# A planner that counts the memory port shared by VectorE and GpSimd, and the last four attention units of batch 0 split from PSUM

## The chip, the cores and the metric

The kernel runs on one core of one Trainium2 chip. The metric is the device time of one execution in microseconds (us). The engines are TensorE (PE, with its weight loads PEld), VectorE (DVE), ScalarE (ACT), GpSimd (POOL) and SyncE (SP), which issues every DMA here. PSUM is the memory into which PE writes; POOL doesn't reach it.

## What is computed

Clustered attention feeds two layers of two matrix products each, all in fp32 (1536 tokens, model width 512, inner width 2048):

```python
# q, k, v: (2, 8, 768, 64); centroids: (8, 16, 64)
q_assign = argmax(q_n @ c_n); k_assign = argmax(k_n @ c_n)      # normalised rows
scores = where(q_assign == k_assign, scale * q @ k.T, -1e9)
x = softmax(scores) @ v                    # to (1536, 512)
h = x @ w_in;   x = (max(h, 0) + alpha * min(h, 0)) @ w_out
h = x @ w_in2;  out = (h * clip(h + 3, 0, 6) / 6) @ w_out2
```

## The kernel before

**High and low halves.** To keep fp32 accuracy, operands are split in a rounded high part and a remainder: a copy to the narrower type writes the high part, a subtraction writes the low part, and a product is three passes of PE. The copies are on ACT, sometimes on DVE; the subtractions are on POOL where the source is in SBUF, and on DVE where it is in PSUM.

**Attention.** A batch (768 tokens) is done by itself: four pairs of heads (p), two heads (j) each, and six units (t) of 128 queries per head, so 48 units per batch. A pair is first prepared: q and k are loaded and transposed by PE (L461), split by ACT and DVE (L472 to L496), multiplied with the centroids (L518), and on DVE and POOL (L531 to L566) turned into the one-hot cluster codes (eq, oh, lg) that SP writes into the operands (L581). V is scaled and split (L590 to L627). A unit then is: scores by PE into a PSUM pair ps (L662), the row limit by DVE (L669), exp by ACT into the SBUF buffer e (L694), high part by ACT (L728), low part by POOL (L732), both transposed by a DMA (turn, L640) into a buffer pt or, in batch 0 only, half an acc buffer, and the product with V by PE (pv, L647). After a pair, xn is made by DVE (L747) and transposed by PE (L759) into x. Two variants exist: every unit of batch 0 with t % 4 == 2 is transposed by PE (L707) and split from PSUM; and in batch 1 the units with t % 3 != 0 do exp in place in PSUM (L676) and are split from there (L681 on ACT, L685 on DVE), without e.

From unit EARLY = 44 of batch 0 on a unit is "late": it takes e from a ring of one buffer, since the four others lie in a pool that is closed to make room for the weights.

**The two layers.** Each batch goes through both layers: products with w_in (L892, into pb or pc), an activation (L900 to L915), a split into g (L918 on ACT, L922 on POOL), products with w_out (L941, L944), sums by DVE (L952 to L970). For batch 0 each weight block of 128x512 arrives as the two words of a 64-bit number (wd) and is turned into fp32 in a buffer wf (two of them) by ACT (L807) and three DVE steps (L812, L819, L825); it is stored to DRAM for batch 1 (L830), copied (L834, ACT) and subtracted (L839, POOL) into w.

**The order.** All of this is written as operations with an engine (or two to choose from, `pick`), a cost in us, the buffers that they read, write and take, and a due time vt. `Planner.plan` (L102) runs them through a list schedule with one clock: at each moment an idle engine takes the ready operation of the smallest (vt, n) whose buffers are free. The result is one fixed order per engine; on the chip each engine follows its own order and waits only for its inputs. An operation with two engines goes to the second only if the first is taken and has at least BACKLOG = 3 operations ready.

```python
U0, PREP0, SPAN0 = 2.2, -23.969, 15.768
T1, DU, PREP1, SPAN1 = 110.562, 3.672, -22.219, 20.627
```

These set the due times: a unit of batch 0 every U0, the layers of batch 0 and the units of batch 1 from T1 on. The attention of batch 1 thus runs between the products of the layers of batch 0, and the layers of batch 1 come last.

Of the kernel before, what the change touches and what calls it, by code (L numbers as in the profile page):

```python
# [27 lines left out]
LOOK = 0  # L28
EARLY = 44
# [32 lines left out]
class Op:  # L62
    __slots__ = ("eng", "dma", "lat", "fn", "vt", "n", "deps", "soft", "outs", "souts", "acq", "rel", "start", "at")


class Planner:
# [7 lines left out]
    def op(self, eng, cost, fn, r=(), w=(), acq=(), vt=0.0, lat=0.2, dma=0.0, after=()):  # L74
        o = Op()
        o.dma = dma
# [25 lines left out]
    def plan(self):  # L102
# [21 lines left out]
        began = set()  # L124
        soon = {e: [] for e in engines}
# [30 lines left out]
        while events:  # L156
            now = events[0][0]
            while events and events[0][0] <= now:
# [7 lines left out]
                for b in ev.rel:  # L166
                    left[id(b)] -= 1
                    if not left[id(b)]:
                        b.ring.live -= 1
                        for a in b.ring.slots[b.slot][1]:  # L170
                            del busy[a]
                            freed[a] = now
            for e in engines:
                if free_at[e] > now:
                    continue
# [3 lines left out]
                while ready[e]:  # L179
# [4 lines left out]
                    if ahead is not None and ahead < o.vt:  # L184
                        put_back.append(item)
                        break
# [24 lines left out]
                    free_at[e] = now + o.eng[e]  # L211
                    seq += 1
# [21 lines left out]
def kernel(  # L234
# [36 lines left out]
    op = P.op  # L271
# [154 lines left out]
    def pick(engs, costs, fn, **kw):  # L426
        o = op(engs, costs, None, **kw)
# [4 lines left out]
    def attention(b, vt_unit, vt_prep, put_x):  # L432
# [3 lines left out]
        def prep(p):  # L436
# [17 lines left out]
            for nm in "qk":  # L454
# [12 lines left out]
                for j in range(2):  # L467
                    a, z = slice(64 * j, 64 * j + 64), slice(64 - 64 * j, 128 - 64 * j)
                    s = st[j]
                    if nm == "q":  # L470
# [12 lines left out]
                        pick(("ACT", "DVE"), (0.84, 0.8), f, r=[(s["qa"], "h"), (s["qa"], "l")],  # L483
                             w=[(s["qb"], "h"), (s["qb"], "m")], vt=v0 + span * 0.5)
                    else:
# [11 lines left out]
                        pick(("ACT", "DVE"), (0.84, 0.8), f, r=[(s["ka"], "h")], w=[(s["ka"], "h2")], vt=vt)  # L497
# [47 lines left out]
            op("DVE", 0.8, f, r=[(lg, 0), (lg, 1), (mx, 0)], w=[(eq, 0)], acq=[eq], vt=vt, lat=0.13)  # L545
# [11 lines left out]
            op("DVE", 0.8, f, r=["desc", (mx, 1)], w=[(eq, 0)], vt=vt, lat=0.13)  # L557
# [11 lines left out]
            for j in range(2):  # L569
                z = slice(64 - 64 * j, 96 - 64 * j)  # L570
                for x, o in (("qb", 32 * j), ("kb", 64 + 32 * j)):
                    if b == 0 and p == 0:
# [4 lines left out]
                        pick(("ACT", "DVE"), (0.84, 0.8), f, r=[(lg, 0), (lg, 1)], w=[(st[j][x], "m")], vt=vt)  # L577
# [46 lines left out]
            pick(("ACT", "DVE"), (0.84, 0.8), f, r=[(vr, 0), (vr, 1)], w=[(v16, 0)], acq=[v16], vt=vt)  # L624
# [3 lines left out]
            pick(("POOL", "DVE"), (1.7, 1.2), f, r=[(vr, 0), (vr, 1), (v16, 0)], w=[(v16, 1)], vt=vt)  # L628
            vts[p] = (v16, vs)

        def head(p, j, vt0):
# [21 lines left out]
            for t in range(NT):  # L653
# [19 lines left out]
                if b and t % 3:  # L673
# [14 lines left out]
                    op("DVE", 0.97, f, r=[ps, (hl, 0)], w=[(hl, 1)], vt=vt)  # L688
# [371 lines left out]
```

## Time and profile before

| what | value |
|---|---|
| median of 3 runs | 831.65 us (825.08 to 832.09) |
| profiled execution, its own time | 829.24 us |
| its span | 827.5 us |
| mean granted TensorE clock | 0.961 of full speed |
| PE, PEld busy | 750.6 us (91%), 694.5 us (84%) |
| DVE, ACT, POOL busy | 522.4 (63%), 470.9 (57%), 482.1 us (58%) |
| DMA | 121.17 MB, 146 GB/s over the span |

The span runs from the first to the last instruction of the profiled execution; its own time has 1.7 us more around it. Busy shares are means over stages of different kinds. PEclk is the share of full speed that TensorE was granted: 1.00 is 2.4 GHz and 0.50 is 1.2 GHz.

### The profile page before, as it was taken

To read this page: it belongs to the slowest core of one execution; us is meant where nothing else is said; L and a number is where in the kernel's file an instruction comes from. 1 tells how busy PE (TensorE), PEld (TensorE's weight loads), DVE (VectorE), ACT (ScalarE), POOL (GpSimd) and SP (SyncE) were. 2 spreads that over 40 slices of the span, in tenths; PEclk is the share of its full clock that TensorE was granted. 3 is DMA by queue.
4 is the path that set the end of the run, shared out by engine and by line. 5 is a ranking of instruction groups with operands and counts; after the bars stand their busy time and mean duration, and the time that the engine had idled before them with its cause. 6 is when DMAs were issued, how large, how long until landed. Compare 5 with 4: busy or idle time off the path is not lost.

```text
span 827.5 us, 14300 instructions
## 1 busy us (share of the span) xinstructions
PE 750.6 (91%) x5337; PEld 694.5 (84%) x5337; DVE 522.4 (63%) x880; ACT 470.9 (57%) x767; POOL 482.1 (58%) x453
## 2 busy tenths in 40 slices
PE   5667877669999989989999999899999999999997
PEld 4556766659999978889889988789999999899986
DVE  7997888879898888988986888621122222122222
ACT  6777859667576676676665554544433254443421
POOL 3685686846654474654764665675565477564630
PEclk9988898859999999998999999999999999999999
DMA  6599989797789999699995564643222131221201
GB/s 131 118 173 217 173 162 197 123 254 191 193 209 230 183 223 235 118 225 206 207 233 183 181 183 160 181 129 111 64 77 63 43 86 51 64 73 55 77 9 69
DMA packets 212965, 121.17 MB, mean 146 GB/s; under 512 B 169504, under 2 KB 189984, under 8 KB 212896
## 3 DMA queue, kind: packets, MB, share of 16 engines
q1 hardware_dynamic: 212896, 120.26, 62.0%
q8 instruction: 41, 0.67, 0.3%
q14 instruction: 28, 0.23, 0.1%
HBM read 61.38 MB, written 21.50 MB: 100 GB/s over the span
## 4 chain that ended last, share of the span: by engine, by line
PE 53%; DVE 19%; DMA 11%; ACT 7%; issue 5%; POOL 4%; SPq 2%; POOLq 0%; ACTq 0%; DVEq 0%
PE pc L892 12%; PE pb L892 9%; PE pb L941 6%; PE pc L941 6%; PE pb L944 6%; PE pc L944 4%; DVE wf L819 4%; PE ps L662 3%; DMA pt<-hl 3%; DVE wf L825 3%; DVE junk L669 3%; PE ps L518 2%; DMA wd<-in_moe_w_in_dram 2%; DMA wd<-in_moe_w_out_dram 2%; DVE wf L812 2%
## 5 line engine op out<-in xcount | busy, mean ns | idle before, releaser
L839 POOL TENSOR_TENSOR w<-wf,w 128x512 fp32r<-128x512 f32 x128 | 168.5, 1319 | 155.2 <-ACT w L834 100.5
L922 POOL TENSOR_TENSOR big<-t,big 128x384 fp32r<-128x384 f32 x128 | 137.8, 1081 | 82.1 <-ACT big L918 76.5
L892 PE MATMUL pc<-xh,w 128*128 128x384 f32 x544 | 150.7, 338 | 1.8 <-DVE vs L613 1.8
L892 PE MATMUL pb<-xh,w 128*128 128x384 f32 x480 | 133.0, 338 | 0.6 <-DVE t L904 0.6
L834 ACT CAST w<-wf 128x512 fp32r<-128x512 f32 x124 | 76.4, 618 | 88.4 <-DVE wf L825 43.0
L732 POOL TENSOR_TENSOR hl<-e,hl 128x768 f16<-128x768 f32 x56 | 96.6, 1732 | 49.6 <-ACT hl L728 40.0
L892 PEld LDWEIGHTS pc<-xh,w 128*128 128x128 f32 x544 | 99.6, 187 | 2.5 <-DVE vs L613 2.1
L669 DVE TENSOR_SCALAR_CACHE_REDUCE junk<-ps 128x768 bf16<-128x768 f32 x96 | 91.0, 948 | 8.9 <-PE ps L662 5.6
L892 PE MATMUL pc<-xl,w 128*128 128x384 f32 x272 | 91.7, 337 | 0.0
L892 PEld LDWEIGHTS pb<-xh,w 128*128 128x128 f32 x480 | 87.8, 188 | 0.9 <-DVE t L904 0.8
L918 ACT CAST big<-t 128x384 fp32r<-128x384 f32 x125 | 63.6, 512 | 42.0 <-DVE t L913 22.8
L944 PE MATMUL pb<-w,big 128*128 128x512 f32 x324 | 79.7, 393 | 2.0 <-POOL big L922 2.0
L892 PE MATMUL pb<-xl,w 128*128 128x384 f32 x240 | 80.9, 337 | 0.0
L941 PE MATMUL pb<-big,w 128*128 128x384 f32 x420 | 80.2, 339 | 0.3 <-ACT t L997 0.3
L662 PE MATMUL ps<-big,big 128*128 128x384 f32 x192 | 60.4, 399 | 21.2 <-DVE big L476 6.3
L941 PEld LDWEIGHTS pb<-big,w 128*128 128x128 f32 x420 | 73.9, 187 | 0.4 <-ACT t L997 0.4
L694 ACT ACTIVATE e<-ps,mn 128x768 f32<-128x768 f32 x64 | 57.3, 904 | 28.4 <-DVE junk L669 26.4
L944 PEld LDWEIGHTS pb<-w,big 128*128 128x128 f32 x324 | 60.3, 188 | 15.7 <-POOL big L922 3.4
L819 DVE SCALAR_TENSOR_TENSOR wf<-wd,wf 128x512 int32<-128x512 int32 x64 | 69.1, 1080 | 1.3
L941 PE MATMUL pc<-big,w 128*128 128x384 f32 x348 | 67.4, 342 | 0.0
L944 PE MATMUL pc<-w,big 128*128 128x512 f32 x252 | 62.4, 394 | 3.7 <-POOL big L922 3.7
L941 PEld LDWEIGHTS pc<-big,w 128*128 128x128 f32 x348 | 62.1, 190 | 0.0
(154 smaller groups left out, 1327.8 us busy)
## 6 DMA issues: line engine op xcount, KB each, us to landing
wd<-in_moe_w_in_dram SPq DMA_DIRECT2D x32, 512.0 KB, 4.6
w<-wf SPq DMA_DIRECT2D x64, 256.0 KB, 3.5
wd<-in_moe_w_out_dram SPq DMA_DIRECT2D x32, 512.0 KB, 4.2
wf<-w SPq DMA_DIRECT2D x64, 256.0 KB, 2.7
raw_q<-in_q_dram SPq DMA_DIRECT2D x16, 192.0 KB, 3.5
raw_k<-in_k_dram SPq DMA_DIRECT2D x16, 192.0 KB, 3.7
raw_v<-in_v_dram SPq DMA_DIRECT2D x16, 192.0 KB, 2.6
out_dram<-acc SPq DMA_DIRECT2D x12, 256.0 KB, 2.0
```

The source lines that it names most:

```text
L662: nc.tensor.matmul(ps.ap[:, kk, 0:NH], s[x].ap[:, i, c0:c0 + 128], s[y].ap[:, kk, :], start=(n == 0), stop=(n == 1))
L669: nc.vector.tensor_scalar(out=junk.rearrange("p (a b) -> p a b", a=2), in0=ps.ap[:, :, 0:NH], scalar1=LN_P, scalar2=None, op0=ALU.add, op1 ...
L694: nc.scalar.activation(out=e.ap.rearrange("p (a b) -> p a b", a=2), in_=ps.ap[:, :, 0:NH], func=ACTF.Exp, bias=mn.ap, scale=-1.0)
L732: tt_on(eng)(out=hl.ap[:, 1, :], in0=e.ap, in1=hl.ap[:, 0, :], op=ALU.subtract)
L819: nc.vector.scalar_tensor_tensor(out=wi, in0=wd.ap[:, :, 1], scalar=-0x80000000, in1=wi, op0=ALU.bitwise_and, op1=ALU.bitwise_or)
L834: copy_on(e)(w.ap[:, 0, :], wf.ap)
L839: tt_on(e)(out=w.ap[:, 1, :], in0=wf.ap, in1=f32(w.ap[:, 0, :]), op=ALU.subtract)
L892: nc.tensor.matmul(hp.ap[:, 0:NH], w.ap[:, hw, 128 * kk:128 * kk + 128], (xl if hx else xh)[i][:, kk, :], start=(m == 0), stop=(m == 3 * K ...
L918: copy_on(e)(g.ap[:, 0, :], t.ap)
L922: tt_on(e)(out=g.ap[:, 1, :], in0=t.ap, in1=f32(g.ap[:, 0, :]), op=ALU.subtract)
L941: nc.tensor.matmul(o.ap[:, 0:NH], w.ap[:, hw, 128 * e:128 * e + 128], g.ap[:, hg, :], start=(m == 0), stop=(m == 3 * FC - 1))
L944: nc.tensor.matmul(o.ap, g.ap[:, hg, 128 * e:128 * e + 128], w.ap[:, hw, :], start=(m == 0), stop=(m == 3 * FC - 1))
```

## The change

The planner gets a resource, the port. An operation on POOL always takes it; an operation on DVE takes it if it is marked `port`: the copies and subtractions that DVE takes over by `pick`, the three steps on wf, and the two comparisons L543 and L556. While the port is taken, such an operation is put back and the next one is tried. The costs of the marked DVE steps are set lower. Two additions are without effect as it stands: no caller uses `hold`, and with HOLD = 0.0 the claim of a waiting DVE operation never holds POOL back. Besides, the late units of batch 0 take the way that two thirds of batch 1 took before: exp in place in PSUM, split from PSUM by ACT and DVE. That includes the one late unit with t % 4 == 2, which PE transposed before.

```diff
-    def op(self, eng, cost, fn, r=(), w=(), acq=(), vt=0.0, lat=0.2, dma=0.0, after=()):
+    def op(self, eng, cost, fn, r=(), w=(), acq=(), vt=0.0, lat=0.2, dma=0.0, after=(), port=False, hold=()):
...
+        for b in hold:
+            if not b.users:
+                o.acq.append(b)
+                b.first = o
+            else:
+                soft.add(b.first)
+            b.users.append(o)
...
+            claim = None
             for e in engines:
                 if free_at[e] > now:
+                    if e == "DVE":
+
+                        claim = min((x for x in ready[e] if self.ops[x[1]].port and x[1] not in began), default=None)
                     continue
...
+                    ported = e == "POOL" or (e == "DVE" and o.port)
+                    if ported and port_free > now:
+                        put_back.append(item)
+                        continue
+                    if e == "POOL" and claim is not None and claim < item and free_at["DVE"] < now + HOLD:
+                        put_back.append(item)
                         break
...
                     free_at[e] = now + o.eng[e]
+                    if ported:
+                        port_free = free_at[e]
...
     def pick(engs, costs, fn, **kw):
+        kw.setdefault("port", True)
         o = op(engs, costs, None, **kw)
...
-            op("DVE", 0.8, f, r=[(lg, 0), (lg, 1), (mx, 0)], w=[(eq, 0)], acq=[eq], vt=vt, lat=0.13)
+            op("DVE", 0.56, f, r=[(lg, 0), (lg, 1), (mx, 0)], w=[(eq, 0)], acq=[eq], vt=vt, lat=0.13, port=True)
...
-                if b and t % 3:
+                if late and (b == 0 or t % 3):
...
-                    op("DVE", 0.97, f, r=[ps, (hl, 0)], w=[(hl, 1)], vt=vt)
+                    o_e = op("DVE", 0.97, f, r=[ps, (hl, 0)], w=[(hl, 1)], vt=vt)
+                    if b == 0:
+                        ps_ops.append(o_e)
...
-                pick(("POOL", "DVE"), (1.7, 1.2), f, r=[e, (hl, 0)], w=[(hl, 1)], vt=vt)
+                pick(("POOL", "DVE"), (1.7, 0.96), f, r=[e, (hl, 0)], w=[(hl, 1)], vt=vt)
...
-            op("DVE", 0.8, g, r=[wd], w=[wf], vt=vt)
+            op("DVE", 0.7, g, r=[wd], w=[wf], vt=vt, port=True)
```

The other pairs of costs change alike (copies on DVE 0.8 to 0.56, subtractions 1.2 to 0.96, the first step on wf 0.55 to 0.43). PE has the same instructions but for six transposes less, POOL three subtractions L732 less; what moves is the order. In the listings of the order each row is one instruction, with its line in its own file (lines after are 24 to 26 higher), the tile written and the tiles read; mn_147 belongs to the 48th unit of batch 0, mn_146 to the 47th.

On ACT, around the exps of these two units (e_115 is the one buffer e, hl_117 and hl_118 are the split results, wf and wd are a weight, the big and the ps under L472 and L487 belong to the second pair of batch 1), before:

```order
L807 ACTIVATE wf_96<-wd_94 128x512
L472 ACTIVATE big_77<-ps_154 64x768
L694 ACTIVATE e_115<-ps_155,mn_146 128x768
L807 ACTIVATE wf_97<-wd_95 128x512
L728 CAST hl_118<-e_115 128x768
L472 ACTIVATE big_79<-ps_154 64x768
L487 CAST big_86<-ps_155 64x768
L487 CAST big_82<-ps_155 64x768
L694 ACTIVATE e_115<-ps_156,mn_147 128x768
L496 CAST big_86<-big_86 64x768
L728 CAST hl_117<-e_115 128x768
```

And after:

```order
L833 ACTIVATE wf_96<-wd_94 128x512
L700 ACTIVATE ps_156<-ps_156,mn_147 128x2x384
L833 ACTIVATE wf_97<-wd_95 128x512
L496 ACTIVATE big_77<-ps_155 64x768
L496 ACTIVATE big_79<-ps_155 64x768
L705 CAST hl_118<-ps_156 128x768
```

The exps are in place in ps, the copy of the 48th unit (hl_118) has come behind the second conversion and the two copies L496 (L472 before).

On SP, the last transposes of batch 0 (into acc; wd are weight loads, w_159 the store of a weight, raw_q and raw_k loads of later pairs of batch 1), before:

```order
L801 DMA wd_94<-in_moe_w_out_dram 128x1024
L830 DMA w_159<-wf_96 128x512
L640 DMA_TRANSPOSE acc_105<-hl_118 128x12x128
L581 DMA big_88<-lg_137 32x768
L581 DMA kb_0_92<-lg_137 32x768
L445 DMA raw_k_99<-in_k_dram 128x6x64
L830 DMA w_159<-wf_97 128x512
L445 DMA raw_k_99<-in_k_dram 128x6x64
L801 DMA wd_95<-in_moe_w_out_dram 128x1024
L640 DMA_TRANSPOSE acc_106<-hl_117 128x12x128
```

And after:

```order
L664 DMA_TRANSPOSE acc_105<-hl_117 128x12x128
L605 DMA big_88<-lg_137 32x768
L605 DMA kb_0_92<-lg_137 32x768
L469 DMA raw_q_98<-in_q_dram 128x6x64
L469 DMA raw_k_99<-in_k_dram 128x6x64
L827 DMA wd_94<-in_moe_w_out_dram 128x1024
L856 DMA w_159<-wf_96 128x512
L469 DMA raw_k_99<-in_k_dram 128x6x64
L664 DMA_TRANSPOSE acc_106<-hl_118 128x12x128
L856 DMA w_159<-wf_97 128x512
```

One weight load and one weight store no longer stand between the rows' first line and the last transpose; a load of q does, and the store of wf_97 has come behind it.

On PE, the cluster products of the first pair of batch 1 (cs) and the products with V of five units of batch 0 (the first from acc_105 or acc_106, the last from pt_107 or pt_108), before:

```order
L647 LDWEIGHTS pt_107
L647 MATMUL pb_158<-v_132,pt_107 128x65
L518 MATMUL ps_155<-big_85,cs 128x384 x2
L518 MATMUL ps_155<-big_89,cs 128x384
L518 MATMUL ps_155<-kb_0_90,cs 128x384
L518 MATMUL ps_155<-big_80,cs 128x384 x2
```

And after:

```order
L542 MATMUL ps_154<-big_76,cs 128x384
L542 MATMUL ps_154<-kb_0_92,cs 128x384
L785 MATMUL pb_157<-ident,xn_136 128x128 x3
L542 MATMUL ps_154<-big_85,cs 128x384 x2
L542 MATMUL ps_154<-big_89,cs 128x384
L542 MATMUL ps_154<-kb_0_90,cs 128x384
L542 MATMUL ps_154<-big_80,cs 128x384 x2
L542 MATMUL ps_154<-big_76,cs 128x384
L542 MATMUL ps_154<-kb_0_92,cs 128x384
L671 LDWEIGHTS acc_105
L671 MATMUL pb_158<-v_132,acc_105 128x65
```

Before, the cluster products followed the last of the five products with V; now the first of the five follows them.

## Rows read from the trace of the kernel before

**Rows 1.** Windows: stretch, its us, busy us of PE PEld DVE ACT POOL, PEclk, DMA, GB/s.

```profile
0.00:187.00 187.00, 131.02 (x1341) 112.72 (x1342) 153.91 (x302) 134.75 (x175) 119.38 (x136) 0.84 0.87 172
187.00:330.00 143.00, 137.88 (x1175) 131.37 (x1174) 128.16 (x216) 96.81 (x158) 80.00 (x76) 1.00 0.92 209
330.00:560.00 230.00, 218.62 (x1427) 200.25 (x1426) 178.91 (x261) 133.53 (x235) 139.38 (x114) 0.99 0.71 183
560.00:828.00 268.00, 263.10 (x1400) 250.14 (x1398) 61.43 (x103) 105.79 (x201) 143.36 (x128) 1.00 0.22 64
```

**Rows 2.** The same view of 3.5 us shortly before the products of L892 begin.

```profile
175.00:178.50 3.50, 0.01 (x1) 0.01 (x1) 1.43 (x5) 2.07 (x3) 1.27 (x1) 0.50 1.25 196
```

**Rows 3.** PE's timeline: start us, us, engine, line, operation [idle before <- releaser].

```profile
144.29 3.04 PE L647 MATMUL pb<-v,acc 128*128 128x65 f16 x72
...
147.72 0.77 PE L518 MATMUL ps<-big,cs 128*128 128x384 f32 x3
...
178.49 1.17 PE L647 MATMUL pb<-v,acc 128*128 128x65 f16 x18 [4.53 <-DMA acc<-hl]
...
182.96 0.88 PE L759 MATMUL pb<-ident,xn 128*128 128x128 f32 x3
...
187.12 0.34 PE L892 MATMUL pc<-xh,w 128*128 128x384 f32 x1
```

**Rows 4.** SP's queue in the timeline, the last transpose of batch 0.

```profile
171.94 2.89 SPq L640 DMA_TRANSPOSE acc<-hl  x1
```

**Rows 5.** The transposes of hl from 150 to 185 us: from issue to landing.

```profile
DMA to landing us min/median/max: 3.7/4.7/6.5
```

**Rows 6.** POOL's timeline.

```profile
154.85 1.28 POOL L839 TENSOR_TENSOR w<-wf,w 128x512 fp32r<-128x512 f32 x1
...
157.68 1.59 POOL L839 TENSOR_TENSOR w<-wf,w 128x512 fp32r<-128x512 f32 x1
159.26 0.83 POOL L561 TENSOR_SCALAR oh<-eq,onoff 128x384 f32<-128x384 bf16 x1
...
166.53 1.65 POOL L732 TENSOR_TENSOR hl<-e,hl 128x768 f16<-128x768 f32 x1 [1.07 <-issue]
```

**Rows 7.** ACT's timeline.

```profile
157.76 0.90 ACT L694 ACTIVATE e<-ps,mn 128x768 f32<-128x768 f32 x1 [0.24 <-POOL hl L732]
159.30 0.67 ACT L807 ACTIVATE wf<-wd 128x512 f32<-128x512 f32 x1 [0.64 <-POOL w L839]
...
160.71 0.81 ACT L472 ACTIVATE big<-ps 64x768 fp32r<-64x768 f32 x1
...
163.79 0.90 ACT L694 ACTIVATE e<-ps,mn 128x768 f32<-128x768 f32 x1
...
165.57 0.83 ACT L728 CAST hl<-e 128x768 f16<-128x768 f32 x1
```

**Rows 8.** DVE's timeline.

```profile
150.86 1.05 DVE L531 STREAM_TRANSPOSE lg<-ps 128x384 f32<-128x384 f32 x2 [3.43 <-ACT v L623]
...
156.88 1.26 DVE L556 TENSOR_TENSOR eq<-desc,mx 128x384 bf16<-128x384 bf16 x1
```

**Rows 9.** Groups by line: out<-in xcount, busy us, mean ns, idle before.

```profile
L819 DVE SCALAR_TENSOR_TENSOR wf<-wd,wf 128x512 int32<-128x512 int32 x64 | 69.1, 1080 | 1.3
...
L825 DVE SCALAR_TENSOR_TENSOR wf<-wd,wf 128x512 uint32<-128x512 uint32 x64 | 57.7, 901 | 0.8
...
L685 DVE SCALAR_TENSOR_TENSOR hl<-ps,hl 128x768 f16<-128x768 f32 x32 | 30.4, 950 | 4.4 <-ACT hl L681 2.8 <-POOL v L627 1.4
...
L681 ACT CAST hl<-ps 128x768 f16<-128x768 f32 x32 | 25.5, 798 | 4.9 <-DMA pt<-hl 4.0 <-DMA acc<-hl 0.9
```

**Rows 10.** L819 alone: ns least, median, most.

```profile
L819 DVE SCALAR_TENSOR_TENSOR wf<-wd,wf x64: 643/694/2121, 46.7 to 526.4; 128x512 int32<-128x512 int32 x64
```

**Rows 11.** One collision, POOL's timeline.

```profile
206.57 1.81 POOL L732 TENSOR_TENSOR hl<-e,hl 128x768 f16<-128x768 f32 x1
```

**Rows 12.** The same stretch, DVE's timeline.

```profile
206.89 2.03 DVE L819 SCALAR_TENSOR_TENSOR wf<-wd,wf 128x512 int32<-128x512 int32 x1
```

More of the change, by code (lines that the diff above doesn't have):

```diff
@@ L28 @@
 LOOK = 0
+HOLD = 0.0
 EARLY = 44
@@ L62 @@
 class Op:
-    __slots__ = ("eng", "dma", "lat", "fn", "vt", "n", "deps", "soft", "outs", "souts", "acq", "rel", "start", "at")
+    __slots__ = ("eng", "dma", "lat", "fn", "vt", "n", "deps", "soft", "outs", "souts", "acq", "rel", "start", "at", "port")
 class Planner:
@@ L482, in f @@
                             copy_on(e)(s["qb"].ap, f32(s["qa"].ap))
-                        pick(("ACT", "DVE"), (0.84, 0.8), f, r=[(s["qa"], "h"), (s["qa"], "l")],
+                        pick(("ACT", "DVE"), (0.84, 0.56), f, r=[(s["qa"], "h"), (s["qa"], "l")],
                              w=[(s["qb"], "h"), (s["qb"], "m")], vt=v0 + span * 0.5)
@@ L496, in f @@
                             copy_on(e)(s["ka"].ap[z], f32(s["ka"].ap[a]))
-                        pick(("ACT", "DVE"), (0.84, 0.8), f, r=[(s["ka"], "h")], w=[(s["ka"], "h2")], vt=vt)
+                        pick(("ACT", "DVE"), (0.84, 0.56), f, r=[(s["ka"], "h")], w=[(s["ka"], "h2")], vt=vt)
             vt = v0 + span * ST[2]
@@ L556, in f @@
                 nc.vector.tensor_tensor(out=eq.ap[:, 0], in0=db, in1=mx.ap[:, :, 1:2].to_broadcast(sh), op=ALU.is_equal)
-            op("DVE", 0.8, f, r=["desc", (mx, 1)], w=[(eq, 0)], vt=vt, lat=0.13)
+            op("DVE", 0.56, f, r=["desc", (mx, 1)], w=[(eq, 0)], vt=vt, lat=0.13, port=True)
             def f():
@@ L576, in f @@
                                        lg.ap[o:o + 32].rearrange("p a b -> p (a b)"))
-                        pick(("ACT", "DVE"), (0.84, 0.8), f, r=[(lg, 0), (lg, 1)], w=[(st[j][x], "m")], vt=vt)
+                        pick(("ACT", "DVE"), (0.84, 0.56), f, r=[(lg, 0), (lg, 1)], w=[(st[j][x], "m")], vt=vt)
                         continue
@@ L623, in f @@
                 copy_on(e)(v16.ap[:, 0, :, :, 0:D], vr.ap)
[L624 removed]
+            pick(("ACT", "DVE"), (0.84, 0.56), f, r=[(vr, 0), (vr, 1)], w=[(v16, 0)], acq=[v16], vt=vt)
             def f(e):
                 tt_on(e)(out=v16.ap[:, 1, :, :, 0:D], in0=vr.ap, in1=v16.ap[:, 0, :, :, 0:D], op=ALU.subtract)
[L628 removed]
+            pick(("POOL", "DVE"), (1.7, 0.96), f, r=[(vr, 0), (vr, 1), (v16, 0)], w=[(v16, 1)], vt=vt)
             vts[p] = (v16, vs)
@@ L813, in g @@
                                         op0=ALU.logical_shift_left, op1=ALU.bitwise_and)
-            op("DVE", 0.55, g, w=[wf], vt=vt, lat=0.13)
+            op("DVE", 0.43, g, w=[wf], vt=vt, lat=0.13, port=True)
             def g():
@@ L820, in g @@
                                                op0=ALU.bitwise_and, op1=ALU.bitwise_or)
-            op("DVE", 0.8, g, r=[wd], w=[wf], vt=vt, lat=0.13)
+            op("DVE", 0.7, g, r=[wd], w=[wf], vt=vt, lat=0.13, port=True)
             def g():
```

8 lines of the change are left out of this document (5 added, 3 removed).

## The prediction

> **What bounds the kernel now.** I read the windows first, then PE's timeline, then the timelines of SP, POOL, ACT and DVE in the stretch that PE's gaps pointed to, and last the groups by line for prices.
>
> The windows [rows 1] show three regimes. From 560 us PE is busy for 263.10 of what is left of the span; that stretch is PE's work and nothing else, and an order of the other engines can give it almost nothing. From 187 to 560 us PE idles 143.00 - 137.88 = 5.1 and 230.00 - 218.62 = 11.4, together 16.5 us of 373. Up to 187 us PE idles 56.0 us and its mean granted clock is 0.84, and no other engine is full either (DVE 153.91 of 187, ACT 134.75, POOL 119.38). That first stretch is a chain of small hand-overs, and it ends when the first product of the first layer (L892) can start, at 187.12 us [rows 3]. From there on PE has enough work to stay filled. So I ask what sets 187.12.
>
> The product needs the whole of x of batch 0, so it needs the last unit of batch 0, the 48th. In PE's timeline its product with V (L647, from an acc buffer, which only batch 0 uses for transposes) starts at 178.49 after a wait of 4.53 us for the transpose; the transposes of x follow from 182.96, then L892 [rows 3]. While PE sits there its granted clock is 0.50, the lower of its two levels, 1.2 GHz [rows 2]. SP issued that transpose at 171.94 [rows 4], and the transposes of this stretch took 3.7 to 6.5 us to land, this one the 6.5 (171.94 to 178.4) [rows 5]. Behind the transpose stands POOL's subtraction L732 of 166.53, over at 168.18 [rows 6]; behind that ACT's copy of 165.57 and exp of 163.79 [rows 7].
>
> Why is that exp so late? The last four units of batch 0 share one buffer e. The exp of the unit before began at 157.76, after a wait for POOL's subtraction of the unit before it [rows 7]: one slot, held through exp, copy and a subtraction on a POOL that also has weights to do. The two exps stand 163.79 - 157.76 = 6.0 us apart.
>
> **The change part by part.** *Last four units from PSUM.* They need neither e nor POOL: exp in place, copy by ACT (0.798) and subtraction by DVE (0.950) [rows 9]. Three subtractions leave POOL (of 1.65 each [rows 6]), four of 0.950 come to DVE, where one from the path through PE's transposes, at about the same price, goes. I cost DVE's extra 3 x 0.95 = 2.9 us at nothing: DVE idles 187 - 153.91 = 33.1 us in this stretch [rows 1]. Without that cover the 2.9 us fall on the path.
>
> I follow the 48th unit through the new order. On ACT (first place shown) its copy now stands behind two conversions of weights (L807) and two copies L472. The conversions wait for the two wf slots, which POOL's L839 frees; in the new order the first four L839 stand together behind the subtraction L561 of oh. That one can start when DVE's L556 is over, at 156.88 + 1.26 = 158.14 [rows 8]; before it started at 159.26 because an L839 of 157.68 was ahead [rows 6]. So: L561 over at 158.14 + 0.83 = 159.0; two L839 of 1.28 [rows 6], over at 160.3 and 161.6; the second conversion, 0.67, over at 162.3; two L472 of 0.81, over at 163.9 [rows 7]; copy 0.80, 164.7; DVE's subtraction 0.95, 165.7 [rows 9]. DVE has five steps on wf and a reduction of raw_v ahead of it, which run while ACT does the same stretch, so I count them as hidden; if one of them meets POOL's lock they cost up to 1.4 us more (2.03 against 0.64 for L819 [rows 10, 12]). On SP (second place) the two last transposes had two weight loads (L801) and two weight stores (L830) around them in the rows shown; now one of each, and a load of q more, stand ahead of the last, and the other store is behind it. Issue at about 165.8 instead of 171.94: **6.2 us earlier**. Bounds: 0, if SP's queue or the 16 DMA engines eat it (their busy share is 1.25 at that time [rows 2]); 9.0, if it also lands in 3.7 instead of 6.5 us [rows 5]. I take the 6.2 alone, since the load on the DMA engines is not changed.
>
> *Eq chain earlier.* In PE's old order five products with V stand ahead of the cluster products L518 of the first pair of batch 1, four of them 3.04 us, and L518 starts at 147.72 [rows 3], while DVE sits idle 3.43 us for their outcome [rows 8]. In the new order (third place) L518 stands ahead of these five. The gain on that chain lies between 0 (if the operands are then late) and 3.4 us; it feeds L556, thus the chain above. I take **1.5 us**, a little nearer to 0, since what L518 reads may then be what is late.
>
> *The port.* With the new rule the planner runs no DVE step with the mark port while POOL works, and the costs of these steps fall to their undisturbed size. What collisions cost can be read: L819 starts 0.32 us after an L732 of 1.81 us and takes 2.03 us, ending 0.54 us after it [rows 11, 12]; over its 64 runs the mean is 1080 against a least of 643 ns, and the like step L825 has 901 [rows 9, 10]. Against 643 that is 64 x 0.437 + 64 x 0.258 = 44.5 us of DVE time. None of it goes because a plan says so: the order is fixed within each engine, and POOL and DVE meet on the chip when their inputs happen to be there. Between 187 and 560 us, where nearly all of it lies, PE has only 16.5 us of idle to give [rows 1]. Bounds: 16.5 us gained if the plan holds on the chip, and the 11.2 us of the slow rival below lost. I take 0, as the steps are as many as before, POOL's too but for three.
>
> The rule in the Trainium skill (SBUF — State Buffer, Who interferes with whom) speaks against the port part: it calls the shared pair a lock that is held for the whole instruction, and says that the order of issue decides who blocks. By that rule an order fixed per engine can shift the waits but not end them, and the sum stays at 821.5; if the plan's order held on the chip, it would be the 813 of the second rival. The collision above agrees with the lock: the DVE step ends 0.54 us after POOL's, most of the 0.643 that it takes alone.
>
> **Sum.** The profiled execution took 829.24 us (span 827.5). Less 6.2, less 1.5, port 0: 829.24 - 7.7 = 821.5 us. Its time lies 2.4 us below the median of the runs shown, 831.65, whose spread is 825.08 to 832.09; so a measurement of this kernel can tell about 1% from no change, 8.3 us. Against the median the forecast is 1.2% faster.
>
> **Rivals.**
> *The start of L892 does not move.* The transpose is ready earlier, but SP's queue and busy DMA engines hold it. For it: the DMA share of 1.25 and a landing of 6.5 us [rows 2, 5]. Against it: a weight load and a weight store have left the queue ahead of it. Then nothing is left but the eq chain, inside the noise: 829 us.
>
> *The plan holds on the chip and the clock stays up.* The collisions go in part, PE's 16.5 us after 187 shrink by half, and PE with fewer gaps before 187 is not left at 0.50. For it: DVE has 128.16 of 143 busy from 187 to 330 [rows 1], so freed DVE time would be felt. Against it: both engines' starts depend on PE and DMA. 821.5 - 8.2 = 813 us.
>
> *Weights late (slower).* The L839 that ran at 154.85 before [rows 6] now stands behind L561 and ends at 160.3, so the third weight's conversion starts 160.3 - 156.1 = 4.2 us later. Four L839 in a row, and more such rows later, also hold the port against the very DVE steps that feed the next weights. If each L819 and L825 met half an L839, 0.64 us, the two would wait 1.28 instead of 0.437 + 0.258 = 0.70 us, 0.58 more per weight. Of the 64 weights, spread to 526.4 us [rows 10], some 24 fall between 187 and 330, where DVE idles 143 - 128.16 = 14.8 us [rows 1]: 24 x 0.58 = 13.9 us fill it, and half of that, 7, would reach PE. 829.24 + 4.2 + 7.0 = 840 us. It decides as soon as weights, not x, come last at the products of the first layer (L892, L941). Against it: PE's gaps after 187 are few, and two weights are converted long before.
>
> **How the numbers follow.** Forecast 821.5: 0.45, with an own range of 815 to 826; start not moved, 829: 0.27; plan holds, 813: 0.13; weights late, 840: 0.15. Range 810 to 837: it takes in 813 with a little below it, and stops short of the slow rival, most of whose 0.15 is what is left out. Faster by over 1%, that is under 823.3: 0.34 of the forecast's 0.45, all of 0.13 and 0.02 of the unmoved, 0.49. Slower by over 1%, above 840.0: 0.10 of the slow rival and 0.03 of the unmoved, 0.13. Within 1%: 0.38.
>
> **What would show it.** Right: the last transpose of an acc buffer issued near 164 to 166 us, L892 starting near 179 to 181, PE idle before that under 52 us, and L819's mean still above 1000 ns. Wrong: L892 starting at 186 or later (unmoved), or PE waiting at the first L941 for ACT's or POOL's weight (weights late), or L819's mean near 700 with PE's idle after 187 halved (plan holds). A gain that shows only after 560 us would refute all of it.

## The result and the profile after

The changed kernel takes 840.13 us in the median of 6 runs (837.48 to 845.45), the kernel before 832.13 us on the same chip (6 runs): a ratio of 1.0102, 95% interval 1.006 to 1.0145. It is 1% slower, 8.5 us, where 7.7 us less was forecast. The profiled execution of after took 845.45 us, the longest of the six, with a span of 843.7 us; differences of a few us between single profiles are therefore not read below, only where they come from. Line numbers of after are those of before plus 24, and plus 26 from the code of the units on (L819 is now L845, L892 is L918, L647 is L671).

The windows of after, cut at the start of L918; the columns are those of [rows 1]:

```profile
0.00:184.00 184.00, 125.16 (x1328) 110.26 (x1329) 149.25 (x301) 132.02 (x172) 111.95 (x132) 0.87 0.89 170
184.00:330.00 146.00, 136.50 (x1097) 130.26 (x1097) 117.58 (x205) 96.78 (x157) 79.99 (x77) 0.96 0.88 195
330.00:560.00 230.00, 216.47 (x1438) 198.60 (x1438) 167.13 (x264) 133.76 (x230) 131.13 (x105) 0.96 0.73 189
560.00:844.00 284.00, 277.98 (x1473) 263.09 (x1471) 65.70 (x110) 112.74 (x215) 153.29 (x138) 1.00 0.22 65
```

Read beside [rows 1], the first stretch became shorter, the last is still nothing but PE's work, and the middle is where the time went. There PE idles 146.00 - 136.50 + 230.00 - 216.47 = 23.0 us, where it was 16.5, and its mean granted clock is 0.96, where it was 1.00 and 0.99. From the first product of the first layer to the first product of batch 1's layers (the 1st and the 769th matmul of L892, now L918, in the traces) it is 187.1 to 543.2 us before and 183.6 to 559.2 after: 356.0 against 375.5, 19.5 us longer. What follows lasts 280.6 and 280.7 us in TensorE's records. So 3.5 us were gained ahead of the layers and 19.5 lost in them while batch 1's attention runs beside them.

In this execution the clock is the larger part of it. The trace of after has seven stretches at a granted clock of 0.50, the lower of the two levels, between 184 and 560 us (from 281, 315, 346, 383, 435, 510 and 547 us; six of 3.4 us and one of 6.8, 27.2 in all); before has one, of 6.8 us. Counted at half, that is 13.6 us lost against 3.4: 10.2 us more. With the 6.5 us more of idle that makes 16.7 of the 19.5. How much of it a median run loses to the clock is not on record, but it is probably less: over the whole execution the profiled run has a mean granted clock of 0.955, the other five runs have 0.961 to 0.967, and 0.006 more of some 840 us is already 5 us less lost.

What PE waited for from 184 to 560 us (engine, tile and line waited for: us in all, times, longest); before, the first four rows:

```profile
PE pc L944 <- POOL big L922: 3.7, 3, 2.0
PE pc L759 <- DVE xn L747: 3.2, 1, 3.2
PE pc L892 <- DVE vs L613: 1.8, 1, 1.8
PE pb L647 <- DVE xn L747: 1.6, 1, 1.6
...
PE pc L647 <- DMA pt<-hl: 0.6, 1, 0.6
...
PE pb L647 <- DMA pt<-hl: 0.3, 1, 0.3
```

And after:

```profile
PE pb L671 <- DMA pt<-hl: 4.6, 3, 1.8
PE pc L785 <- DVE xn L773: 3.3, 2, 2.2
PE pc L671 <- DMA pt<-hl: 2.8, 3, 1.3
...
PE pc L970 <- POOL w L865: 1.8, 2, 1.1
PE ps L686 <- ACT e L720: 1.7, 3, 1.2
PE pb L970 <- POOL w L865: 1.7, 1, 1.7
PE pb L785 <- DVE xn L773: 1.5, 2, 1.1
PE pb L970 <- ACT w L860: 1.3, 1, 1.3
```

Two kinds of wait are new: 7.4 us for transposes of probabilities, where it was 0.9, and waits of the output product L970 for weights, where there were none. One of them in PE's timeline of after, with the wait behind it:

```profile
313.21 0.72 PE L671 MATMUL pb<-v,pt 128*128 128x65 f16 x18 [1.79 <-DMA pt<-hl]
314.26 0.62 PE L686 MATMUL ps<-big,big 128*128 128x384 f32 x2 [0.33 <-ACT e L720]
...
318.64 0.69 PE L785 MATMUL pc<-ident,xn 128*128 128x128 f32 x2 [2.18 <-DVE xn L773]
```

The windows of the same stretch:

```profile
309.00:311.40 2.40, 2.40 (x14) 2.09 (x13) 1.82 (x3) 1.82 (x3) 2.40 (x3) 1.00 1.06 290
311.40:315.20 3.80, 1.69 (x24) 1.54 (x24) 2.25 (x4) 3.34 (x5) 0.51 (x1) 0.99 0.96 273
315.20:322.00 6.80, 4.62 (x18) 4.11 (x17) 5.57 (x11) 4.90 (x9) 5.13 (x4) 0.50 0.52 131
322.00:326.00 4.00, 4.00 (x29) 3.84 (x28) 2.81 (x3) 2.98 (x5) 2.89 (x3) 1.00 0.71 189
```

Before that stretch PE was full at 1.00. Then it stood 1.79 us for a transpose and 0.33 us for an exp, and was busy for 1.69 of 3.80 us; from 315.20 on it has 6.8 us at 0.50, and within them it stood another 2.18 us for xn. DVE makes xn from that very product with V, but had other steps in front of it, and one of these, L851, met an instruction of POOL, the kind of collision that the rule is to prevent. In POOL's timeline and in DVE's:

```profile
315.44 1.64 POOL L758 TENSOR_TENSOR hl<-e,hl 128x768 f16<-128x768 f32 x1 [3.54 <-issue]
...
315.56 2.07 DVE L851 SCALAR_TENSOR_TENSOR wf<-wd,wf 128x512 uint32<-128x512 uint32 x1
```

A wait for pt and, within some 6 us of it, a second wait stand at five of the seven half-speed stretches in after: at 311 and 316 (the second inside the stretch), 342 and 344, 374 and 380, 432 and 434, and 271 and 278 us. The second wait is for xn in three of them, for an exp (342) and for kb (271) in the others; that the first wait made the second one late is not shown. A single wait can stand there too: in before the one stretch at 0.50 begins within the 3.2 us for xn of the list above. Ahead of the last two (510 and 547) stand three and two waits of L970 for weights, each group within 4 us.

DVE did get what the port rule is for. The groups by line of after, to be read beside [rows 9]:

```profile
L851 DVE SCALAR_TENSOR_TENSOR wf<-wd,wf 128x512 uint32<-128x512 uint32 x64 | 57.3, 895 | 0.9
L845 DVE SCALAR_TENSOR_TENSOR wf<-wd,wf 128x512 int32<-128x512 int32 x64 | 52.3, 818 | 0.7
L838 DVE TENSOR_SCALAR wf<-wf 128x512 int32<-128x512 int32 x64 | 39.3, 615 | 27.1 <-ACT wf L833 27.1
```

The step on wf that took 1080 ns in the mean takes 818, and DVE is busy for 499.7 us instead of 522.4. DVE has less to do, and the kernel is slower.

### The profile page after: what moved, and what is told of

Same layout as the page of the kernel before. It is cut to its first block, busy times and chain, and to the rows that moved or that the text cites. A ratio compares the mean times of both kernels' runs of the same rounds, so it can differ in the third digit from the quotient of the medians.

```text
span 843.7 us, 14275 instructions
## 1 busy us (share of the span) xinstructions
PE 756.1 (90%) x5331; PEld 702.2 (83%) x5331; DVE 499.7 (59%) x877; ACT 475.3 (56%) x772; POOL 476.4 (56%) x451
## 4 chain that ended last, share of the span: by engine, by line
PE 66%; DVE 9%; DMA 8%; POOL 6%; ACT 5%; issue 4%; SPq 0%; POOLq 0%; DVEq 0%; ACTq 0%
PE pc L918 14%; PE pb L918 13%; PE pc L970 8%; PE pc L967 8%; PE pb L967 7%; PE pb L970 7%; PE ps L686 3%; DMA pt<-hl 3%; PE ps L542 2%; DVE junk L693 2%; POOL hl L758 2%; PE pb L671 2%; DMA raw_v<-in_v_dram 1%; DMA w<-wf 1%; POOL raw_v L642 1%
## 5 line engine op out<-in xcount | busy, mean ns | idle before, releaser
L918 PE MATMUL pc<-xh,w 128*128 128x384 f32 x520 | 142.5, 340 | 0.0
L918 PE MATMUL pb<-xh,w 128*128 128x384 f32 x504 | 137.3, 339 | 0.0
L758 POOL TENSOR_TENSOR hl<-e,hl 128x768 f16<-128x768 f32 x53 | 88.0, 1675 | 56.9 <-ACT hl L754 30.9
L693 DVE TENSOR_SCALAR_CACHE_REDUCE junk<-ps 128x768 bf16<-128x768 f32 x96 | 91.2, 950 | 17.4 <-PE ps L686 14.0
L918 PEld LDWEIGHTS pc<-xh,w 128*128 128x128 f32 x520 | 95.6, 189 | 0.3
L918 PEld LDWEIGHTS pb<-xh,w 128*128 128x128 f32 x504 | 92.2, 187 | 0.3
L918 PE MATMUL pc<-xl,w 128*128 128x384 f32 x260 | 88.1, 339 | 0.0
L918 PE MATMUL pb<-xl,w 128*128 128x384 f32 x252 | 85.1, 338 | 0.0
L970 PE MATMUL pc<-w,big 128*128 128x512 f32 x300 | 74.8, 403 | 2.5 <-POOL w L865 1.8
L967 PE MATMUL pc<-big,w 128*128 128x384 f32 x384 | 74.6, 346 | 0.0
L967 PE MATMUL pb<-big,w 128*128 128x384 f32 x384 | 74.5, 347 | 0.0
L970 PE MATMUL pb<-w,big 128*128 128x512 f32 x276 | 68.7, 400 | 4.9 <-POOL big L948 1.9
L970 PEld LDWEIGHTS pc<-w,big 128*128 128x128 f32 x300 | 57.9, 194 | 16.1 <-POOL w L865 2.6
L967 PEld LDWEIGHTS pc<-big,w 128*128 128x128 f32 x384 | 70.3, 194 | 0.0
L967 PEld LDWEIGHTS pb<-big,w 128*128 128x128 f32 x384 | 70.2, 194 | 0.0
L671 PEld LDWEIGHTS <-pt 128*128 128x128 f16 x1296 | 46.9, 101 | 26.4 <-DMA pt<-hl 14.2
L970 PEld LDWEIGHTS pb<-w,big 128*128 128x128 f32 x276 | 52.3, 192 | 17.7 <-POOL big L948 3.1
```

Of the source, the lines that this page charges most:

```text
L671: nc.tensor.matmul(o.ap[:, DO * t:DO * t + DO], pt.ap[:, hp * NT + kt, :], v16.ap[:, hv, j, kt, 0:DO], start=(kt == 0 and n == 0), stop=(k ...
L693: nc.vector.tensor_scalar(out=junk.rearrange("p (a b) -> p a b", a=2), in0=ps.ap[:, :, 0:NH], scalar1=LN_P, scalar2=None, op0=ALU.add, op1 ...
L758: tt_on(eng)(out=hl.ap[:, 1, :], in0=e.ap, in1=hl.ap[:, 0, :], op=ALU.subtract)
L918: nc.tensor.matmul(hp.ap[:, 0:NH], w.ap[:, hw, 128 * kk:128 * kk + 128], (xl if hx else xh)[i][:, kk, :], start=(m == 0), stop=(m == 3 * K ...
L967: nc.tensor.matmul(o.ap[:, 0:NH], w.ap[:, hw, 128 * e:128 * e + 128], g.ap[:, hg, :], start=(m == 0), stop=(m == 3 * FC - 1))
L970: nc.tensor.matmul(o.ap, g.ap[:, hg, 128 * e:128 * e + 128], w.ap[:, hw, :], start=(m == 0), stop=(m == 3 * FC - 1))
```

## The experiments

All kernels were compared with the kernel before on the same chip, five rounds each. The two right columns are from each profile's window 187 to 560 us (before: 356.50 and 0.99), which is one execution.

| kernel | port rule | late units from PSUM | new costs | slack | ratio, 95% interval | PE busy us | PEclk |
|---|---|---|---|---|---|---|---|
| after | both sides | yes | yes | | 1.0102, 1.0060 to 1.0145 | 349.97 | 0.96 |
| e1 | | yes | | | 0.9936, 0.9909 to 0.9962 | 355.73 | 0.99 |
| e2 | both sides | | yes | | 1.0105, 1.0059 to 1.0151 | 351.04 | 0.97 |
| e3 | both sides | | | | 1.0201, 1.0171 to 1.0232 | 345.06 | 0.94 |
| e4 | | | yes | | 0.9983, 0.9959 to 1.0007 | 354.82 | 0.99 |
| e5 | | yes | yes | | 0.9942, 0.9919 to 0.9966 | 353.51 | 1.00 |
| e6 | DVE waits | yes | yes | | 1.0039, 1.0014 to 1.0063 | 347.29 | 0.96 |
| e7 | POOL waits | yes | yes | | 0.9993, 0.9968 to 1.0017 | 352.85 | 1.00 |
| e8 | both, DVE stands still | yes | yes | | 1.0073, 1.0049 to 1.0097 | 354.19 | 0.98 |
| e9 | both sides | yes | yes | both | 0.9963, 0.9940 to 0.9986 | 353.06 | 0.98 |
| e10 | | yes | yes | both | 0.9939, 0.9910 to 0.9967 | 354.17 | 0.98 |
| e11 | both, due time moved | yes | yes | | 1.0072, 1.0041 to 1.0104 | 353.15 | 0.97 |
| e12 | none, due time moved | yes | yes | | 0.9936, 0.9910 to 0.9963 | 351.11 | 1.00 |
| e13 | DVE lengthened | yes | yes | | 0.9988, 0.9963 to 1.0014 | 352.55 | 0.99 |
| e14 | half the time | yes | yes | | 0.9962, 0.9938 to 0.9987 | 355.76 | 0.99 |
| e15 | both sides | yes | yes | transposes | 0.9996, 0.9975 to 1.0017 | 351.87 | 0.97 |
| e16 | both sides | yes | yes | weights | 1.0078, 1.0052 to 1.0105 | 349.35 | 0.97 |

**Which part of the change.** e1 is the kernel before with the late units alone; e2, e3 and e4 leave these out.

```diff
 e1, from before:
-                if b and t % 3:
+                if late and (b == 0 or t % 3):
...
 e2, from after:
-                if late and (b == 0 or t % 3):
+                if b and t % 3:
 e3, from e2, and so at the other places with a cost of DVE:
-                pick(("ACT", "DVE"), (0.84, 0.56), f, r=[e], w=[(hl, 0)], acq=[hl], vt=vt)
+                pick(("ACT", "DVE"), (0.84, 0.8), f, r=[e], w=[(hl, 0)], acq=[hl], vt=vt)
 e4, from e2:
-                    ported = e == "POOL" or (e == "DVE" and o.port)
+                    ported = False
```

> The kernel before with the last four units of batch 0 split from PSUM, planner and costs as before. Theory A (the planner part makes the loss: an order with less slack, in which PE waits more often between 184 and 560 us and then works at half clock for a while; the late units gain about 3.5 us at the start of L892): 828 to 830 us, ratio to before 0.995 to 0.998, L892 starting at 182 to 184 us. Theory B (the late units make the loss): 840 us, ratio 1.01. Theory C (any new order scatters by about 1%, whichever part made it): no pattern, this one anywhere from 824 to 842.

> The changed planner with its port and its new costs, the last four units of batch 0 as before. Theory A: 840 to 844 us, ratio 1.01 to 1.015, with at least five stretches at half clock between 184 and 560 us. Theory B: 832, ratio 1.0. Theory C: anywhere from 824 to 844, and not the sum of what the next two runs show.

> The port as a resource, but the costs of before and the late units as before. Theory A, if the port rule is what takes the slack: 838 to 842 us, and DVE's busy time near the 500 us of after instead of 522. If the lower costs take it: 832 and DVE near 520. Theory C: no relation to the run before.

> The new costs, but no port in the plan, late units as before. Theory A with the lower costs at fault (the plan believes DVE's weight steps to be 15 to 30% shorter than before, while on the chip they take 615 to 895 ns): 838 to 845 us, DVE busy 520 or more, PE waiting for weights. With the port rule at fault: 832. Theory C: no relation to the runs before.

The late units alone gain 0.6%, the planner's part alone loses as much as the whole change, and within it the new costs cost nothing: it is the port rule. The parts don't add: with the rule in force (after against e2) the gain of the late units is not to be seen. With the old costs, which lie above those of undisturbed steps (0.8 us for L819, whose median is 694 ns [rows 10]), the rule loses 2.0%; with the new ones 1.05%. Theory A's numbers were met only in part: e1 gained more than it wanted (0.9936 for 0.995 to 0.998), e2's profile has four stretches at half clock where at least five were expected, and e3 lost more (849 us for 838 to 842).

**The whole change without the port rule, and its two sides.**

```diff
 e5, from after:
-                    ported = e == "POOL" or (e == "DVE" and o.port)
+                    ported = False
 e6, from after (in the plan only DVE's marked steps wait):
-                    if ported and port_free > now:
+                    if ported and e == "DVE" and port_free > now:
 e7, from after (only POOL waits):
-                    if ported and port_free > now:
+                    if ported and e == "POOL" and port_free > now:
 e8, from after (a marked step that finds the port taken is not passed over by DVE's other work):
                         put_back.append(item)
+                        if e == "DVE":
+                            break
                         continue
```

> The changed kernel with its late units and its new costs, but a plan that knows no port. Theory D (the port rule in the plan is the whole loss, late units and costs are each a little to the good): 825 to 830 us, ratio 0.99 to 0.996, PE idle between the start of L892's products and 580 us 15 to 18 us, at most two stretches at half clock there. Rival (the late units stop helping once the costs are changed, the parts don't add): 832 to 838.

> The changed kernel, but in the plan only DVE's marked steps wait for the port; POOL starts whatever DVE does. Theory E (the loss comes from DVE's side: while POOL works in the plan, DVE takes other work in front of the steps on the weights and these come late on the chip): 838 to 845 us, time from the first conversion on ACT to DVE's last step on a weight longer than the 5.0 to 7.5 us of before in the second to fifth group of eight weights. Theory F (the loss comes from POOL's side, whose operations the plan puts off): 826 to 833.

> The changed kernel, but in the plan only POOL waits for the port; DVE's marked steps start whatever POOL does. Theory E: 826 to 833 us. Theory F: 838 to 845 us.

> The changed kernel with the port, but in the plan a DVE whose next operation finds the port taken stays idle until it is free; it does not pass over that operation to take a later one. Theory E in its form that passing over is the harm: 827 to 834 us, weight steps no longer apart than before. If holding DVE at all is the harm (the plan then runs ahead with PE's side and leaves no slack for transposes and weights): 838 or more, since DVE loses still more time in the plan.

One line changed (ported = False) takes the kernel from 1.0102 to 0.9942; the port rule costs 1.6% of the time. Neither side makes that alone: from 0.9942, the wait on DVE's side costs 1.0% and that on POOL's 0.5%, so neither theory E nor F has both of its numbers. The profiles add something to these totals. From the first product L918 to the end of PE's last matmul it is 643.5 us in e5, 642.5 in e7, 659.6 in e6 and 656.3 in after: in the layers, by these single profiles, the wait on DVE's side loses as much as the whole rule, and that on POOL's nothing. In e6 L918 starts at 172.65, 11.0 us earlier than in after, and so its total is smaller; in e7 it starts at 183.09, 3.3 us later than in e5, and that is about what it loses. That marked steps are passed over is not the harm either: DVE standing still in the plan gives 1.0073. In e5 the first part came out as it was forecast for after; that is taken up below. Its collisions are those of before (L845 at 1024 ns in the mean, [rows 9] 1080; DVE busy 522.9 us), and its window from 187 to 560 us is at a clock of 1.00:

```profile
187.00:560.00 373.00, 353.51 (x2570) 325.95 (x2567) 301.58 (x474) 227.33 (x388) 218.48 (x189) 1.00 0.79 193
```

PE waits for transposes in e5 too, but no second wait stands close behind the longest of them (1.50 us at 203.3, 1.58 at 332.0), where waits come near each other they are shorter (0.98 and 1.41 us at 269.9 and 275.2), and there is no stretch at half speed between 184 and 560 us:

```profile
PE ps L686 <- ACT e L720: 3.2, 3, 1.5
PE pb L671 <- DMA pt<-hl: 3.2, 4, 1.5
...
PE pc L671 <- DMA pt<-hl: 2.6, 4, 1.6
```

In sum these waits for transposes are 5.8 us, not far from the 7.4 of after; their sum does not tell the two kernels apart.

**Just in time, scatter, or the time held.** e9 keeps the port rule and gives the plan slack; e11 and e12 move a due time that has nothing to do with the port, with and without the rule; e14 holds the port for half the time.

```diff
 e9, from after:
-                return op("SP", 1.3, f, r=[(hl, 0), (hl, 1)], w=[(pt, 0), (pt, 1)], acq=[pt], vt=vt, dma=2.3, lat=0.95)
+                return op("SP", 1.3, f, r=[(hl, 0), (hl, 1)], w=[(pt, 0), (pt, 1)], acq=[pt], vt=vt, dma=2.3, lat=2.5)
-        pick(("POOL", "DVE"), (1.3, 0.68), g, r=[wf, (w, 0)], w=[(w, 1)], vt=vt)
+        pick(("POOL", "DVE"), (1.3, 0.68), g, r=[wf, (w, 0)], w=[(w, 1)], vt=vt, lat=1.5)
 e11, from after, and e12, from e5:
-T2, LEAD, LOADS = 329.488, 19.217, 14.435
+T2, LEAD, LOADS = 329.488, 19.9, 14.435
 e14, from after:
-                        port_free = free_at[e]
+                        port_free = now + 0.5 * o.eng[e]
```

> The changed kernel with more slack in the plan: a transpose of probabilities is planned to arrive 1.55 us later (2.5 in place of 0.95) and a weight's second half 1.3 us later (1.5 in place of 0.2), so that TensorE's order asks for both later than before. Theory G (the port rule leaves a plan whose arrivals are just in time, and TensorE waits on the chip for transposes and weights; slack mends it): 0.994 to 1.000 of the kernel before. Theory I (the held time is the harm: the marked steps are pushed back in VectorE's order behind the units' work, the weights come late whatever slack is asked for): 1.007 to 1.013, as the changed kernel's 1.0102. Theory H (scatter between orders): anything from 0.99 to 1.01.

> The changed kernel with one due time moved by 0.7 us that has nothing to do with the port (LEAD 19.9 in place of 19.217). Theory H (the loss is the scatter between any two orders): anything from 0.99 to 1.01, without regard to the port rule. Theories G and I (the port rule makes the loss): 1.007 to 1.014.

> The kernel with the late units from PSUM and the new costs but without the port rule, with the same due time moved by 0.7 us. Theory H: anything from 0.99 to 1.01. Theories G and I: 0.992 to 0.998, as without the shift (0.9942).

> The changed kernel whose plan holds the port for half the planned time of an instruction. Theory I (loss grows with the time held, whole hold +1.6%): half to a quarter of the loss is left, 0.996 to 1.002, with 185 to 560 us some 5 to 10 us shorter than in the changed kernel. Theory H: anything from 0.99 to 1.01. A yes-or-no effect of any hold would leave 1.007 or more.

Slack takes the loss away (0.9963) with the port rule fully in force: theory G is borne out, and theory I, by which the steps come late whatever slack is asked for, falls. DVE has still fewer collisions in e9 than in after (busy 495.3 us, L838 at 561 ns in the mean), and that gains nothing over e5 (0.9942), which has all of them. Scatter falls as well: the moved due time leaves the two kinds of plan where they were, 1.0072 and 0.9936. With half the hold almost nothing of the loss is left; the effect is not in proportion to the time held, and not a matter of any hold at all. Its 0.9962 lies at the edge of what theory I wanted, so it is e9 and not e14 that decides against I. The half hold also thins the collisions less: L845 takes 942 ns in the mean, where after has 818 and e5 1024.

**Which arrivals, and whether slack helps any plan.** e10 is e5 with both slacks, e15 and e16 are after with the first and the second line of e9's slack alone. In e13 POOL never waits in the plan, and DVE's step starts and lasts longer by what is left of POOL's.

```diff
 e13, from after:
-                    if ported and port_free > now:
-                        put_back.append(item)
-                        continue
...
-                    if ported:
+                    if e == "DVE" and o.port and port_free > now:
+                        free_at[e] += port_free - now
+                    if e == "POOL":
                         port_free = free_at[e]
```

> The late units from PSUM, the new costs, no port rule, and both slacks (transposes 1.55 us, weights 1.3 us later in the plan). Theory G (slack mends what the port rule spoils): little changes without the rule, 0.992 to 0.997, as 0.9942 without slack. Theory J (slack helps every plan alike, and the port rule's cost stands): as much better as the changed kernel became with slack (1.4%), 0.978 to 0.984.

> The changed kernel with slack for the transposes of probabilities alone. Theory G1 (the transposes were just in time): 0.994 to 1.000. Theory G2 (the weights were): 1.006 to 1.012, as the changed kernel. If both count: 1.000 to 1.006.

> The changed kernel with slack for the weights' second halves alone. Theory G1 (transposes): 1.006 to 1.012. Theory G2 (weights): 0.994 to 1.000. If both count: 1.000 to 1.006.

> The changed kernel with another port rule in the plan: GpSimd never waits, and VectorE's marked step starts at once and is planned longer by what is left of GpSimd's instruction. Theory K (the harm is the pushing back of steps, not that the port is counted): 0.994 to 0.999, as without the rule. Theory G (the harm is that a plan which counts collisions has its arrivals just in time): between the rule on VectorE's side alone (1.0039) and the changed kernel, 1.001 to 1.010.

The control decides against theory J: without the port rule slack changes nothing (0.9939 against 0.9942), so it mends what the rule spoils. Slack for the transposes alone takes most of the loss away (0.9996), slack for the weights alone none that can be told from after (1.0078): G1. The waits from 184 to 560 us say the same. With slack for the weights (e16):

```profile
PE pb L671 <- DMA pt<-hl: 8.7, 3, 3.9
PE pc L671 <- DMA pt<-hl: 3.4, 3, 2.2
```

With slack for the transposes (e15):

```profile
PE ps L686 <- DMA kb<-lg: 6.1, 1, 6.1
PE pb L785 <- DVE xn L773: 3.8, 1, 3.8
...
PE pb L671 <- DMA pt<-hl: 0.2, 1, 0.2
```

The 7.4 us of after are 12.1 in e16 and 0.2 in e15, whose profile has other waits in their place (PE idles 21.1 us from 187 to 560 us, in after 23.0). Shown is thus that slack for the transposes gives most of the time back; that the time is lost in these very waits is argued. The transposes themselves are no slower: the DMAs of hl in the window 187 to 560 us land after these times (from issue; least, median, most), in e16, which has the longest waits,

```profile
DMA to landing us min/median/max: 3.7/4.4/6.8
```

and in e15

```profile
DMA to landing us min/median/max: 3.7/4.9/7.6
```

What differs is how much time PE's order leaves them. From the first matmul of a unit's scores to its first product with V, over the 48 units of batch 1 in the records of PE, the mean is 16.0 us before, 15.9 in e5, 15.1 in after, 14.8 in e16, but 17.4 in e15, 17.3 in e9 and 18.0 in e10. The mean alone doesn't decide, though: e14 has 15.2 and e1 15.4, and both gain; it may matter which units are short. e13 lands at 0.9988: inside what theory K wants (0.994 to 0.999) and beside what G wanted, though its interval reaches both. A rule that lengthens DVE's step instead of pushing it back costs 0.5% against e5, about a third of the 1.6% of the port rule; it gains nothing.

## Why the prediction was wrong

*The late units: the path right, the size half of it.* For the 48th unit the forecast had ACT's copy over at 164.7, DVE's subtraction at 165.7 and SP's issue at 165.8. In after the subtraction was over even earlier, in DVE's timeline:

```profile
163.89 0.94 DVE L709 SCALAR_TENSOR_TENSOR hl<-ps,hl 128x768 f16<-128x768 f32 x1
```

But SP, in its timeline, issued the transpose at 169.09:

```profile
163.90 1.33 SPq L605 DMA_DIRECT2D big<-lg  x1
165.28 0.58 SPq L605 DMA_DIRECT2D kb<-lg  x1
...
168.43 0.55 SPq L469 DMA_DIRECT2D raw_k<-in_k_dram  x1
169.09 5.28 SPq L664 DMA_TRANSPOSE acc<-hl  x1
```

Seven transfers stood ahead of it in SP's queue, from 163.90 to 169.09, at 0.42 to 1.33 us of issue each; the prediction named what left the queue and what came, but did not sum the issue times of all that stood there. Its own rows held that delay: before, POOL's subtraction is over at 168.18 and the transpose is issued at 171.94, 3.8 us later [rows 4, 6]; the chain for the new order gave SP 0.1 us, and in after it took 4.3. So 2.85 of the 6.2 us (6.1 by its own 165.8) came (171.94 to 169.09), and L918 started 3.5 us earlier, at 183.64 instead of 187.12 [rows 3]. The bound named for this step ("0, if SP's queue ... eat it") was half of what happened. In e5, whose plan differs only in the port rule, the same transpose was issued at 165.63 and L918 started at 179.75, beside the 165.8 and the 179 to 181 of the forecast. In the timelines of DVE, SP and PE in e5:

```profile
163.27 0.95 DVE L709 SCALAR_TENSOR_TENSOR hl<-ps,hl 128x768 f16<-128x768 f32 x1
...
165.63 1.79 SPq L664 DMA_TRANSPOSE acc<-hl  x1
...
179.75 0.67 PE L918 MATMUL pc<-xh,w 128*128 128x384 f32 x1
```

That is partly luck: ACT's order in e5 is not the one that the forecast followed, the subtraction was over 1.5 us before the forecast's 165.7, and SP's queue took 1.4 us of it back. The whole gain of e5 is 0.6% (833.38 x 0.0058 = 4.8 us; e1: 5.3), against 7.7 forecast; of the 7.4 us by which L918 starts earlier in the profiles, not all reached the end.

*The eq chain: about as forecast.* The comparison L556, now L580, was over at 157.16 in after and at 156.36 in e5 instead of 158.14 [rows 8]: 1.0 and 1.8 us earlier, where 1.5 was taken. What that gave to the end can't be told apart from the late units; no run had it alone.

*The port: this step failed.* The prediction said "None of it goes because a plan says so: the order is fixed within each engine", and took 0, with 11.2 us lost as the worse bound. Both halves are refuted. Collisions did go: L845's mean fell to 818 ns where "still above 1000" was to show the step right, and DVE's busy time fell by 22.7 us. And the term is not 0 but a loss of about 833 x 0.016 = 13 us, beyond that bound. With the 7.7 - 4.8 = 2.9 us by which the first two terms were too large that is 16 us, the whole distance from the forecast (-7.7) to the result (+8.5). What was overlooked is that the rule makes the planner believe POOL and DVE slower, and that PE's order comes from the same plan: by the runs with slack, the products with V stand too close to where the plan expects the transposes. Shown are the loss by the rule (e5 against after) and that margin for the transposes takes most of it away, with the rule (e15, e9) and not without it (e10); how the time is lost, wait by wait, is argued from single profiles. The rule quoted from the Trainium skill (SBUF — State Buffer, Who interferes with whom) held no answer to this: an order fixed per engine did not only shift the collisions but thinned them, and by the prediction's own reading of that rule (the plan holds, 813 us) the time should have fallen. The error was to ask only what DVE's time is worth, and not what the same plan does to PE.

*The base.* The sum starts from the profiled run's 829.24 us, 2.4 below the median of before, so 0.3 of the forecast's 1.2% came from no term. Its 7.7 us are 0.9%.

*The rivals.* "Weights late (slower)" named the measured time, 840 us, but not its cause: PE did not wait for a weight at the first L967, steps L845 met POOL less often and not more, and slack for the weights alone left the loss in place. The waits of L970 for weights at 505 to 509 and 544 to 548 us, 5.5 us in after, are its true part. "The plan holds on the chip" came true for the collisions, and its premise that freed DVE time would be felt fell. "L892 does not move" was half right, by SP's queue, as it said. The point that would have shown "plan holds" (a mean near 700 ns with PE's idle halved) was split: the mean fell, the idle grew.

*What stays open.* Why the half hold (e14) loses nothing although its units have as little time as after's, and how the loss divides between the idle and the clock in a median run, since each profile is one execution: e15's has 0.97 and e9's 0.98 in this window at no loss against before. The clock of all runs does not order the kernels either: its mean over the whole execution is 0.962 in after and in e9, 0.959 in e15, 0.969 in e5 and 0.957 in before (31 runs beside e9). So the slack did not work by giving the clock back, as far as these means tell; they take in the first stretch, where most of before's loss by the clock lies. Whether the old costs lose more with the rule (e3) for the same reason was not tried with slack.

The versions that beat both kernels are those without the rule, e1 (0.9936), e12 (0.9936), e10 (0.9939) and e5 (0.9942), and behind them one with a weaker rule (e14) and one with slack (e9); their intervals overlap. e4 (0.9983) can't be told from before.

## What to carry to other kernels

A planner's model is not only a list of costs: whatever makes one engine look later moves the instructions of all the others, and the engine that sets the end must be given margin against what really lands late. Before a shared port is counted in a plan, ask whether the engine that waits for it is the one that limits; here 23 us less of DVE's time bought nothing. In the profile of after, the waits of TensorE that stood close together went with two thirds as much again in clock as in idle (13.6 us on some 21). When a step is said to be issued earlier, sum the issue times of everything that now stands ahead of it in that queue.

## What was not expected of the hardware

The clock's share. In e5 PE idled 19.5 us of the window 187 to 560 us (373 - 353.51) and kept 1.00. In after it idled 23.0 us, and the waits that came close together, 21 us in all, stood at seven stretches at 0.50 that took another 13.6 us. So in these two executions 3.5 us more of idle went with 13.6 us lost by the clock, and a list of waits alone understates what they can cost. It is not the whole of the loss: after's profiled run is the one with the lowest clock of its six, and e9, with the same mean clock over its runs as after, is 1.4% faster.
